# Decay attention and two MoE layers on one core: other homes and order for the first block's loads, and the second block's first steps placed behind the first products

## The chip, the cores and the metric

The kernel runs on 1 core of one Trainium2 chip (trn2). The metric is the device time of one execution in microseconds, the median of 3 runs. The inputs lie in the chip's memory, the weights as float64 numbers whose bytes the kernel converts itself.

## What is computed

```python
# q, k, v: (4 batches, 8 heads, 576, 64); f: (4, 8, 576)
scores = 1.0 / np.sqrt(64) * np.matmul(q, k.transpose(0, 1, 3, 2))
cum = np.cumsum(np.log(np.clip(f, 0.0001, 1.0)), axis=-1)
scores = np.where(causal, -1e9, scores + cum[:, :, :, None] - cum[:, :, None, :])
attn = exp(scores - max) / (sum + 1e-09)
x = np.matmul(attn, v) -> (2304 tokens, 512)
h = x @ w_in                      # 512 x 2048
x = np.maximum(0.01 * h, h) @ w_out   # 2048 x 512
out = ((x @ w_a) * (x @ w_b)) @ w_out2   # 512 x 1536, 1536 x 512
```

## The kernel before

**The work.** Products of the MoE layers run on TensorE in fp32r. Each operand is split into a high and a low part (xh and xl, w[:, 0] and w[:, 1]), and a product is three matmuls: high by high, low by high, high by low. The first MoE works on chunks of 256 tokens. For one chunk and one pair of weight groups (there are 16 groups, 8 pairs), l1 makes h_0, h_1, ... (L857, 24 matmuls of 128x256), ScalarE makes gh (L868) and hs (L869), VectorE gl (L871), and l2 adds to y (L886, 24 matmuls). Weights arrive in raw_a (L156), and ScalarE and VectorE turn them from bytes to fp32 and split them (c_a, w_a: L120, L125 on ScalarE, L121, L130, L167, L168 on VectorE).

**The attention.** It goes block by block; a block is a batch and a part of its tokens. The first block is tokens 0 to 255 of batch 0, the second the rest of batch 0. Heads come in pairs (0 to 3): both heads of a pair lie side by side in the 128 partitions. For a pair the steps are: load q, k (xq, xk), v (vn) and the scan of the logarithms (cumb); transpose q and k on TensorE (tq, tk) and copy them (qn, kn); scores on TensorE (s); the decay and the causal mask on GpSimd (p); scores and decay added with a row minimum on VectorE (L374); exp on ScalarE (L345); normalisation; transpose of the probabilities (pp) and a copy (ph); product with v (av); and the result split into xh (ScalarE) and xl (VectorE). The first chunk of the MoE is the first block's result, so h_0 needs xh and xl of all four pairs; the innermost loop of l1 begins with pair 3.

**What sets the order.** The first block's order is a list of words, FIRST (from L613): `lq0` loads q of pair 0, `lk`, `lv`, `lc` load k, v and the scan, `g1` a group of weights, `qT`, `kT` are the transposes, `Sa`, `Sb` scores, `D` the decay, `m` the mask, `M` the sum and minimum, `E` exp, `N` the normalisation, `T`, `h` the probabilities' transpose and copy, `V` the product with v, `xh`, `xl` the split, `ca` to `cf` the conversion of a group. InOrder (L593) chains each engine's instructions in this order, in_line (L145) the loads on SyncE's queue (L642 is `load`). In the text below V3 is the word V of pair 3, four matmuls in the order (eight records in the trace). The listed loads have high priority; other instructions are placed by a scheduler, by priority. Behind (L80) is a wrapper of an engine: each instruction given through it stands behind one instruction (`first`) in that engine's order. In the second block, heads 2 to 7 go through pe_held (behind the last matmul of h_0) and dve_held (behind xl of pair 3); heads 0 and 1 go free.

**Homes.** A tile's tag names its place in memory. Before, q of pairs 0 and 2 share the tag xq, pairs 1 and 3 xq2; the same holds for k (xk, xk2) and v (vs, vhl). So a load for pair 2 waits until pair 0's reader has finished, and the second block's tiles follow in the same tags.

Of the kernel before, what the change touches and what calls it, by code (L numbers as in the profile page):

```python
# [26 lines left out]
def kernel(  # L27
# [570 lines left out]
    class InOrder:  # L598
# [19 lines left out]
        cc0 kn0 Sa0 qn1 cd0 kT1 lq3 lk3 g3 lc3 D011 D001 Sb0 m011 m010 kn1 m001 ce0 M010 M000 M011 ca1 M001
        cf0 Sa1 D100 E011 Sb1 m100 D110 E010 M100 cb1 E000 D101 E001 D111 rec01 cc1 rec00 m101 qT2 N01 m110
        m111 kT2 N00 qn2 T01 M111 ca2 g4 kn2 T00 M110 D200 M101 E110 cb2 D211 Sa2 E111 m211 cd1 E101 Sb2  # L620
        D201 E100 m201 h01 qT3 D210 rec11 h00 m200 kT3 N10 m210 cc2 N11 V0 lv2 M200 M201 E200 M211 E201 M210
        ce1 T11 E211 D310 D300 qn3 kn3 T10 D301 E210 cf1 xh0 Sa3 m310 h11 m301 m300 Sb3 h10 xl0 D311 ca3 g5
        rec21 m311 M300 V1 lv3 N21 M310 E300 M311 E310 M301 E311 N20 T21 xh1 rec31 E301 T20 N31 h21 xl1 T31
        cd2 h20 V2 rec30 ce2 N30 cb3 T30 xh2 h31 xl2 h30 cc3 V3 cd3 xh3 xl3 cf2 ce3 cf3
# [221 lines left out]
    def l1(i, pr):  # L846
# [5 lines left out]
        for u in range(2):  # L852
            wih, wil = wa[2 * pr + u][0], wa[2 * pr + u][1]
            n = 0
            for c in reversed(range(ND)):
# [303 lines left out]
```

## Time and profile before

| | |
|---|---|
| median of 3 runs | 1079.65 us (1077.82 to 1080.82) |
| the profiled execution | 1078.16 us |
| its span in the profile | 1076.3 us |
| busy: PE, DVE, ACT, POOL | 1049.8, 553.8, 544.1, 205.3 us |
| mean granted clock of TensorE | 0.992 of full speed |

The span is counted from the first to the last instruction of the profiled execution; 1.86 us of its time lie outside. PE is TensorE (PEld its weight loads), DVE VectorE, ACT ScalarE, POOL GpSimd, SP SyncE, which only issues transfers here. A wait in brackets stands at the instruction that follows it and names what ended it. DMA rows of the chain of waits run from issue to landing.

### The profile page before, as it was taken

How to read it: one execution, taken by the hardware profiler on the slowest of the kernel's cores; microseconds unless marked ns; L12 is line 12 of the kernel's file. 1: busy time of each engine (PE TensorE's matmuls, PEld its weight loads, DVE VectorE, ACT ScalarE, POOL GpSimd, SP SyncE). 2: the span in 40 equal slices, each digit the busy share in tenths (PEclk: the TensorE clock that was granted, in tenths of full speed). 3: DMA queues.
4: the chain of work that ended last, by engine and by line, in shares of the span. 5: the costliest groups of instructions: out<-in, count | busy, mean ns of one | idle time of the engine just before them, and what ended most of it. 6: DMA issues, size and time to landing. Idle time of an engine off the chain costs nothing.

```text
span 1076.3 us, 19114 instructions
## 1 busy us (share of the span) xinstructions
PE 1049.8 (98%) x6945; PEld 944.0 (88%) x6945; DVE 553.8 (51%) x1290; ACT 544.1 (51%) x1212; POOL 205.3 (19%) x430
## 2 busy tenths in 40 slices
PE   5799999999999999999999999999999999999998
PEld 3577789999999999999999988888888888888897
DVE  5599767877788777767428684112112111211121
ACT  7588777967887868877435562112112111211121
POOL 4435323343343324233000001010002000100000
PEclk9799999999999999999999999999999999999999
DMA  8788245233553244321236662002001000100010
GB/s 239 198 259 239 44 93 113 48 92 67 103 105 66 64 87 105 77 51 34 79 98 206 224 196 59 1 5 75 1 1 50 20 1 1 50 0 1 1 40 20
DMA packets 185438, 86.40 MB, mean 80 GB/s; under 512 B 143808, under 2 KB 173248, under 8 KB 185344
## 3 DMA queue, kind: packets, MB, share of 16 engines
q1 hardware_dynamic: 179728, 79.34, 28.4%
q10 hardware_dynamic: 5616, 5.84, 1.6%
q8 instruction: 55, 0.90, 0.4%
q14 instruction: 39, 0.32, 0.1%
HBM read 75.63 MB, written 9.51 MB: 79 GB/s over the span
## 4 chain that ended last, share of the span: by engine, by line
PE 92%; DMA 3%; DVE 2%; issue 1%; POOL 0%; ACT 0%; SPq 0%; ACTq 0%; DVEq 0%; POOLq 0%
PE ab L955 27%; PE h L857 18%; PE y L886 18%; PE o L978 14%; PE s L76 5%; PE av L76 5%; PE pp L76 3%; DMA raw_a<-in_moe_w_out_dram 1%; DMA xq_f<-in_q_dram 1%; DVE c_a L130 0%; DMA vn_f<-in_v_dram 0%; DMA cumb_f<-cum_dram 0%; POOL p L390 0%; DVE p L90 0%; PE av_f L608 0%
## 5 line engine op out<-in xcount | busy, mean ns | idle before, releaser
L955 PE MATMUL ab<-yh,w_ab 128*128 128x512 f32 (+1 forms) x960 | 279.5, 367 | 0.0
L857 PE MATMUL h<-xh,w_a 128*128 128x256 f32 x1152 | 228.6, 284 | 1.2 <-ACT hs L869 1.2
L886 PE MATMUL y<-gh,w_a 128*128 128x256 f32 x1152 | 223.3, 282 | 1.6 <-ACT gh L868 1.6
L955 PEld LDWEIGHTS ab<-yh,w_ab 128*128 128x128 f32 x960 | 174.2, 188 | 30.4
L857 PEld LDWEIGHTS h<-xh,w_a 128*128 128x128 f32 x1152 | 185.3, 190 | 6.1 <-ACT hs L869 2.0
L961 DVE TENSOR_TENSOR p<-ab,p 128x512 f32<-128x512 f32 (+1 forms) x60 | 38.3, 638 | 291.0 <-PE ab L955 291.0
L886 PEld LDWEIGHTS y<-gh,w_a 128*128 128x128 f32 x1152 | 182.3, 188 | 5.4 <-ACT gh L868 2.2
L955 PE MATMUL ab<-yl,w_ab 128*128 128x512 f32 (+1 forms) x480 | 176.2, 367 | 0.0
L857 PE MATMUL h<-xl,w_a 128*128 128x256 f32 x576 | 163.1, 283 | 0.1
L886 PE MATMUL y<-gl,w_a 128*128 128x256 f32 x576 | 160.9, 281 | 0.1
L978 PE MATMUL o<-w_c,pph 128*128 128x512 f32 x432 | 142.7, 389 | 0.0
L960 ACT COPY p<-ab 128x512 f32<-128x512 f32 (+1 forms) x60 | 32.6, 544 | 179.9 <-PE ab L955 179.3
L857 PEld LDWEIGHTS h<-xl,w_a 128*128 128x128 f32 x576 | 109.3, 190 | 0.7 <-DVE xl L429 0.3
L886 PEld LDWEIGHTS y<-gl,w_a 128*128 128x128 f32 x576 | 108.3, 188 | 1.2 <-DVE c_a L121 0.5
L955 PEld LDWEIGHTS ab<-yl,w_ab 128*128 128x128 f32 x480 | 90.2, 188 | 15.3
L362 POOL TENSOR_SCALAR p<-cumb,ncum_t 128x384 f32<-128x384 f32 (+1 forms) x112 | 77.0, 695 | 138.1 <-PE pp L76 39.1
L111 ACT CAST pph<-p 128x512 fp32r<-128x512 f32 (+1 forms) x60 | 34.6, 577 | 127.7 <-DVE p L961 127.7
L978 PEld LDWEIGHTS o<-w_c,pph 128*128 128x128 f32 x432 | 81.1, 188 | 16.6
L345 ACT ACTIVATE p<-p,stat 128x384 f32<-128x384 f32 (+4 forms) x128 | 77.0, 603 | 33.8 <-DVE stat L374 25.0
L112 POOL TENSOR_TENSOR yl<-sy,yh 128x512 fp32r<-128x512 f32 (+1 forms) x16 | 19.2, 1210 | 390.0 <-ACT yh L111 252.9
L978 PE MATMUL o<-w_c,ppl 128*128 128x512 f32 x216 | 84.2, 390 | 0.0
L871 DVE TENSOR_TENSOR gl<-hs,gh 128x512 fp32r<-128x512 f32 x72 | 51.0, 708 | 41.6 <-ACT hs L869 41.1
(155 smaller groups left out, 1655.8 us busy)
## 6 DMA issues: line engine op xcount, KB each, us to landing
cumb<-cum_dram SPq DMA_DIRECT2D x32, 288.0 KB, 3.8
raw_a<-in_moe_w_out_dram SPq DMA_DIRECT2D x15, 511.6 KB, 5.9
raw_a<-in_moe_w_in_dram SPq DMA_DIRECT2D x15, 510.5 KB, 4.7
raw_c<-in_moe_w_out_dram SPq DMA_DIRECT2D x12, 511.6 KB, 5.3
raw_ab<-in_moe_w_a_dram SPq DMA_DIRECT2D x12, 510.5 KB, 5.7
raw_ab<-in_moe_w_b_dram SPq DMA_DIRECT2D x12, 510.5 KB, 6.6
xq<-in_q_dram SPq DMA_DIRECT2D x144, 32.0 KB, 2.1
y_dram<-yo ACTq DMA_DIRECT2D x18, 256.0 KB, 2.9
```

The costliest lines, as they stand in the source:

```text
L76: return method(*args, **kw)
L111: nc.scalar.copy(hi, src)
L112: (lo_engine or nc.gpsimd).tensor_tensor(out=lo, in0=src, in1=f32(hi), op=ALU.subtract)
L345: act_att.activation(pt, pt, AF.Exp, bias=stat[:, 0, s : s + 1], scale=-1.0, accum_out=stat[:, 1, s : s + 1])
L362: made = pool_att.tensor_scalar(pt, cumb[:, :n], 1.0, ncum_t[:, t, bh : bh + 1], op0=ALU.mult, op1=ALU.add)
L857: made = nc.tensor.matmul(hps[:, u, :], w[:, c * P : c * P + P], x[:, c, :], start=(n == 0), stop=(n == 3 * ND - 1))
L871: nc.vector.tensor_tensor(out=gl, in0=hs, in1=f32(gh), op=ALU.subtract)
L886: nc.tensor.matmul(o, w[:, d * P : d * P + P], g[:, u, :], start=(fi == 0 and n == 0 and d % 2 == 0), stop=(fi == NF1 - 1 and n == 2 and d ...
L955: nc.tensor.matmul(o[:, :tn], w[:, c * P : c * P + P], y[:, c, :tn], start=(m == 0), stop=(m == 3 * ND - 1))
L960: nc.scalar.copy(p[:, :tn], ab[0][:, :tn])
L961: nc.vector.tensor_tensor(out=p[:, :tn], in0=ab[1][:, :tn], in1=p[:, :tn], op=ALU.mult)
L978: nc.tensor.matmul(o, g[:, t * P : t * P + P], w, start=(fi == 0 and m == 0), stop=(fi == NF2 - 1 and m == 2))
```

## The change

There are three parts.

**Homes.** A new function `pairs` gives one tile to two pairs each of k (ks_f0, ks_f1) and v (vs_f0, vs_f1), in the tags that held one pair; q of pairs 2 and 3 gets a tile in the tag `tk` (qs_f1), in which the scan's ones lay. No load of the first block shares a place with another pair's tile any more.

**The loads' order.** All loads stand at the list's head, ahead of the first computing word; the computing words keep their order.

**The second block's heads 0 and 1.** Three new wrappers: pe_next and act_next (behind the last matmul of V3, and behind xh of pair 3) take the transposes of q and of the first half of k and their copies; pe_mid (behind the last matmul of h_0's first half) takes the transposes of k's second half and the scores.

```diff
-    pe_held, dve_held = Behind(pe_free), Behind(dve_free)
+    pe_held, dve_held, pe_next, act_next, pe_mid = (
+        Behind(e) for e in (pe_free, dve_free, pe_free, act_att, pe_free)
+    )
     def engines_of(b, r, h):
-        return (pe_held, dve_held) if (b, r) == (0, 1) and h >= 2 else (pe_free, dve_free)
+        if (b, r) != (0, 1):
+            return pe_free, dve_free, act_att
+        return (pe_held, dve_held, act_att) if h >= 2 else (pe_next, dve_free, act_next)
...
-        pe_att, dve_att = engines_of(b, r, h)
+        pe_att, dve_att, act_att = engines_of(b, r, h)
+        pe_late = pe_mid if pe_att is pe_next else pe_att
...
-                        pe_att.transpose(tk[:, ...
+                        (pe_late if c0 else pe_att).transpose(tk[:, ...
...
-                    pe_att.matmul(o[:n, u, : cols_.stop - cols_.start], ...
+                    pe_late.matmul(o[:n, u, : cols_.stop - cols_.start], ...
...
     FIRST = """
-        lq0 lk0 lq1 lk1 g1 cumT ncum lc1 lv0 g2 ca0 rep qT0 cb0 D000 D010 kT0 lq2 lk2 lc2 lv1 m000 qn0 qT1
+        lq0 lk0 lq1 lk1 g1 cumT ncum lv0 lk2 lq2 lc1 g2 lc2 lv1 lq3 lk3 lc3 g3 lv2 lv3 ca0 rep qT0 cb0 D000
...
+        def pairs(p, key, tags):
+            both = tile_of((key, p // 2), lambda: ap_.tile([P, 2, 2, 2, 64], F32, tag=tags[p // 2], name=f"{key}_f{p // 2}"))
+            return both[:, p % 2]
         def lq(p):
-            x = got["xq", p] = ap_.tile([P, 2, 2, 64], F32, tag=("xq", "xq2")[p % 2], name=f"xq_f{p}")
+            if p < 2:
+                x = ap_.tile([P, 2, 2, 64], F32, tag=("xq", "xq2")[p], name=f"xq_f{p}")
+            else:
+                x = pairs(p, "qs", (None, "tk"))
+            got["xq", p] = x
         def lk(p):
-            x = got["xk", p] = ap_.tile([P, 5, 2, 64], F32, tag=("xk", "xk2")[p % 2], name=f"xk_f{p}")
+            x = got["xk", p] = pairs(p, "ks", ("xk", "xk2"))
         def lv(p):
-            x = got["v", p] = ap_.tile([P, 5, 2, 64], F32, tag=("vs", "vhl")[p % 2], name=f"vn_f{p}")
+            x = got["v", p] = pairs(p, "vs", ("vs", "vhl"))
...
+            got["av", "end"] = made
...
             dve_held.first = made
+            pe_next.first, act_next.first = got["av", "end"], got["xh", p]
...
-                    if pe_held.first is None and u == 1 and n == 3 * ND - 1:
-                        pe_held.first = made
+                    for late_, half in ((pe_mid, 0), (pe_held, 1)):
+                        if late_.first is None and u == half and n == 3 * ND - 1:
+                            late_.first = made
```

On SyncE's queue, behind the loads of pairs 0 and 1's q and k and the first weights, there stood before (a digit behind `_f` is the pair, raw_a_2 and raw_a_3 are weight groups; v of pairs 2 and 3 followed some 20 rows on):

```order
L642 DMA cumb_f1_127<-cum_dram_58 128x256 x2
L642 DMA vn_f0_130<-in_v_dram 128x2x64 x2
L156 DMA raw_a_2_133<-in_moe_w_in_dram 128x4x1021
L156 DMA raw_a_2_133<-in_moe_w_out_dram 128x4093
L642 DMA xq_f2_153<-in_q_dram 128x2x64 x2
L642 DMA xk_f2_156<-in_k_dram 128x2x64 x2
L642 DMA cumb_f2_159<-cum_dram_58 128x256 x2
L642 DMA vn_f1_162<-in_v_dram 128x2x64 x2
L642 DMA xq_f3_184<-in_q_dram 128x2x64 x2
L642 DMA xk_f3_187<-in_k_dram 128x2x64 x2
L156 DMA raw_a_3_190<-in_moe_w_in_dram 128x4x1021
L156 DMA raw_a_3_190<-in_moe_w_out_dram 128x4093
```

Now there stands (vs_f0 and ks_f1 are the tiles of two pairs, 0 and 1 or 2 and 3):

```order
L647 DMA vs_f0_126<-in_v_dram 128x2x64 x2
L647 DMA ks_f1_129<-in_k_dram 128x2x64 x2
L647 DMA qs_f1_132<-in_q_dram 128x2x64 x2
L647 DMA cumb_f1_135<-cum_dram_58 128x256 x2
L160 DMA raw_a_2_138<-in_moe_w_in_dram 128x4x1021
L160 DMA raw_a_2_138<-in_moe_w_out_dram 128x4093
L647 DMA cumb_f2_141<-cum_dram_58 128x256 x2
L647 DMA vs_f0_126<-in_v_dram 128x2x64 x2
L647 DMA qs_f1_132<-in_q_dram 128x2x64 x2
L647 DMA ks_f1_129<-in_k_dram 128x2x64 x2
L647 DMA cumb_f3_150<-cum_dram_58 128x256 x2
L160 DMA raw_a_3_153<-in_moe_w_in_dram 128x4x1021
L160 DMA raw_a_3_153<-in_moe_w_out_dram 128x4093
L647 DMA vs_f1_156<-in_v_dram 128x2x64 x4
```

The q and k of pair 2 have moved ahead of the scan rows of pair 1 (cumb_f1) and of the weights raw_a_2, the scan rows of pair 3 ahead of raw_a_3, and all v have come up to the other loads.

On PE, around V3 (av_f3) and the first product (h_0_0; names with `0_1_0` are the second block's heads 0 and 1), there stood before:

```order
L608 MATMUL pp_f3_0_462<-ident_65,p_f3_0_357 128x128 x3
L76 MATMUL tq_0_1_0_586<-ident_65,xq_0_1_0_576 128x128 x2
L76 MATMUL tq_0_1_0_586<-ident_65,xk_0_1_0_577 128x64
L76 MATMUL tk_0_1_0_0_591<-ident_65,xk_0_1_0_577 128x128 x2
L608 MATMUL av_f3_473<-ph_f3_0_470,vn_f3_411 64x256
L76 MATMUL tk_0_1_0_2_595<-ident_65,xk_0_1_0_577 128x128 x2
L76 MATMUL tk_0_1_0_2_595<-ident_65,xk_0_1_0_577 128x64
L608 MATMUL av_f3_473<-ph_f3_1_467,vn_f3_411 64x256
L608 MATMUL av_f3_473<-ph_f3_0_470,vn_f3_411 64x128
L608 MATMUL av_f3_473<-ph_f3_1_467,vn_f3_411 64x128
L76 MATMUL s_0_1_0_2_609<-kn_0_1_0_575,qn_0_1_0_574 128x384 x2
L857 MATMUL h_0_0_485<-xh_0_370,w_a_0_211 128x256
```

Now there stands:

```order
L613 MATMUL pp_f3_0_457<-ident_65,p_f3_0_355 128x128 x3
L613 MATMUL av_f3_468<-ph_f3_0_465,vs_f1_156 64x256
L613 MATMUL av_f3_468<-ph_f3_1_462,vs_f1_156 64x256
L613 MATMUL av_f3_468<-ph_f3_0_465,vs_f1_156 64x128
L613 MATMUL av_f3_468<-ph_f3_1_462,vs_f1_156 64x128
L76 MATMUL tq_0_1_0_581<-ident_65,xq_0_1_0_571 128x128 x2
L76 MATMUL tq_0_1_0_581<-ident_65,xk_0_1_0_572 128x64
L76 MATMUL tk_0_1_0_0_586<-ident_65,xk_0_1_0_572 128x128 x2
L873 MATMUL h_0_0_480<-xh_0_368,w_a_0_212 128x256
```

V3 is no longer divided, and of the second block only the transposes tq and the first tk stand ahead of the first product.

Right behind the 24 matmuls of h_0 there now stands on PE:

```order
L76 MATMUL tk_0_1_0_2_590<-ident_65,xk_0_1_0_572 128x128 x2
L76 MATMUL tk_0_1_0_2_590<-ident_65,xk_0_1_0_572 128x64
L76 MATMUL tq_0_1_2_629<-ident_65,xq_0_1_2_619 128x128 x2
L76 MATMUL tq_0_1_2_629<-ident_65,xk_0_1_2_620 128x64
L76 MATMUL tk_0_1_2_0_634<-ident_65,xk_0_1_2_620 128x128 x2
L903 MATMUL y_0_0_542<-gh_0_0_506,w_a_0_212 128x256
L903 MATMUL y_0_1_543<-gh_0_0_506,w_a_0_212 128x256
L873 MATMUL h_0_1_511<-xh_0_368,w_a_2_452 128x256
```

The second tk has moved here. The first head's matmul of s_0_1_0_2 follows behind the last matmul of h_1 (h_0_1), and the second head's behind 22 matmuls of y more; both stood ahead of h_0 before.

## Rows read from the trace of the kernel before

**Rows 1.** The page's busy times; share of the span, number of instructions.
```profile
PE 1049.8 (98%) x6945; PEld 944.0 (88%) x6945; DVE 553.8 (51%) x1290; ACT 544.1 (51%) x1212; POOL 205.3 (19%) x430
```

**Rows 2.** By stretch: us, busy (instructions) by engine, granted clock, DMA share, GB/s.
```profile
10.00:20.00 10.00, 5.03 (x23) 2.58 (x21) 7.38 (x25) 7.16 (x16) 5.45 (x12) 1.00 1.00 290
...
40.00:45.00 5.00, 3.61 (x13) 1.72 (x15) 0.88 (x1) 0.73 (x3) 0.08 (x1) 0.50 0.95 265
...
60.00:120.00 60.00, 57.28 (x396) 44.02 (x394) 56.87 (x117) 51.71 (x100) 29.94 (x36) 1.00 0.73 205
120.00:142.00 22.00, 22.00 (x155) 17.45 (x155) 13.10 (x39) 13.46 (x35) 5.75 (x15) 0.93 0.18 39
150.00:250.00 100.00, 100.00 (x837) 99.26 (x836) 76.31 (x216) 79.26 (x202) 36.07 (x90) 1.00 0.41 87
```

**Rows 3.** Chain of waits, first 60 us: start us, us, what.
```profile
8.33 4.73 DMA raw_a<-in_moe_w_out_dram
...
13.08 6.32 DMA xq_f<-in_q_dram
...
22.89 4.70 DMA cumb_f<-cum_dram
...
36.41 4.85 DMA vn_f<-in_v_dram
...
42.48 0.92 PE tk L76 x3
...
44.86 1.58 PE s L76 x4
```

**Rows 4.** PE timeline: start us, us, instructions, [idle before and releaser].
```profile
19.54 0.66 PE L608 MATMUL tqk_f<-ident,xq_f 128*128 128x128 f32 x2 [3.05 <-DMA xq_f<-in_q_dram]
...
35.30 1.96 PE L608 MATMUL av_f<-ph_f,vn_f 128*64 128x256 f32 x8 [0.79 <-DVE c_a L608]
...
41.39 1.08 PE L608 MATMUL av_f<-ph_f,vn_f 128*64 128x256 f32 x2 [1.96 <-DMA vn_f<-in_v_dram]
...
46.38 0.58 PE L857 MATMUL h<-xh,w_a 128*128 128x256 f32 x1
46.76 0.41 PE L857 MATMUL h<-xl,w_a 128*128 128x256 f32 x1
...
48.03 0.32 PE L857 MATMUL h<-xl,w_a 128*128 128x256 f32 x1
...
49.95 0.28 PE L857 MATMUL h<-xh,w_a 128*128 128x256 f32 x1
```

**Rows 5.** POOL timeline, same columns.
```profile
22.24 1.87 POOL L608 TENSOR_SCALAR p_f<-cumb_f,ncum_t 128x128 f32<-128x128 f32 x1
...
27.78 2.23 POOL L608 TENSOR_SCALAR p_f<-cumb_f,ncum_t 128x128 f32<-128x128 f32 x3 [3.18 <-DMA cumb_f<-cum_dram]
```

**Rows 6.** DVE timeline, same columns.
```profile
22.73 1.22 DVE L608 SCALAR_TENSOR_TENSOR c_a<-raw_a,c_a 128x1024 int32<-128x1024 int32 x1
...
30.78 0.29 DVE L608 CUSTOM_DVE_ANT_0 p_f<-s_f,p_f 128x128 f32<-128x128 f32 x1 [1.00 <-POOL p_f L608]
...
45.30 0.43 DVE L608 TENSOR_TENSOR xl<-av_f,xh 128x256 fp32r<-128x256 f32 x1 [4.43 <-ACT xh L608]
...
49.93 0.56 DVE L374 CUSTOM_DVE_ANT_0 p<-s,p 128x384 f32<-128x384 f32 x1 [0.90 <-POOL p L365]
```

**Rows 7.** ACT timeline, same columns.
```profile
37.56 1.10 ACT L608 COPY ph_f<-pp_f 128x384 f32<-128x384 f32 x2
...
44.90 0.37 ACT L608 CAST xh<-av_f 128x256 fp32r<-128x256 f32 x1 [1.04 <-PE av_f L608]
```

**Rows 8.** PE timeline around 92 us, upper clock level.
```profile
91.95 0.92 PE L76 MATMUL s<-kn,qn 64*128 64x384 f32 x4
92.79 0.64 PE L76 MATMUL tk<-ident,xk 128*128 128x128 f32 x3
```

**Rows 9.** PE timeline, the longest wait between 60 and 142 us.
```profile
119.18 0.50 PE L886 MATMUL y<-gh,w_a 128*128 128x256 f32 x2 [1.62 <-ACT gh L868]
```

More of the change, by code (lines that the diff above doesn't have):

```diff
@@ L273, in att_scores @@
                         w = min(P, nk - c * P)
-                        pe_att.transpose(tk[:, (c - c0) * P : (c - c0) * P + w], xk[:w, c, :, :].rearrange("p u d -> p (u d)"), ident[:w, :w])
+                        (pe_late if c0 else pe_att).transpose(tk[:, (c - c0) * P : (c - c0) * P + w], xk[:w, c, :, :].rearrange("p u d -> p (u d)"), ident[:w, :w])
                     k1 = min(c1 * P, nk)
@@ L282, in scores_of_both @@
                     n, at = min(P, nq - z), slice(u * 64, u * 64 + 64)
-                    pe_att.matmul(o[:n, u, : cols_.stop - cols_.start], qn[at, z : z + n], kn[at, cols_], start=True, stop=True)
+                    pe_late.matmul(o[:n, u, : cols_.stop - cols_.start], qn[at, z : z + n], kn[at, cols_], start=True, stop=True)
             q_at = 0
@@ L616 @@
     FIRST = """
-        lq0 lk0 lq1 lk1 g1 cumT ncum lc1 lv0 g2 ca0 rep qT0 cb0 D000 D010 kT0 lq2 lk2 lc2 lv1 m000 qn0 qT1
[L618 to L624, printed above, removed]
+        lq0 lk0 lq1 lk1 g1 cumT ncum lv0 lk2 lq2 lc1 g2 lc2 lv1 lq3 lk3 lc3 g3 lv2 lv3 ca0 rep qT0 cb0 D000
+        D010 kT0 m000 qn0 qT1 cc0 kn0 Sa0 qn1 cd0 kT1 D011 D001 Sb0 m011 m010 kn1 m001 ce0 M010 M000 M011
+        ca1 M001 cf0 Sa1 D100 E011 Sb1 m100 D110 E010 M100 cb1 E000 D101 E001 D111 rec01 cc1 rec00 m101 qT2
+        N01 m110 m111 kT2 N00 qn2 T01 M111 ca2 g4 kn2 T00 M110 D200 M101 E110 cb2 D211 Sa2 E111 m211 cd1
+        E101 Sb2 D201 E100 m201 h01 qT3 D210 rec11 h00 m200 kT3 N10 m210 cc2 N11 V0 M200 M201 E200 M211 E201
+        M210 ce1 T11 E211 D310 D300 qn3 kn3 T10 D301 E210 cf1 xh0 Sa3 m310 h11 m301 m300 Sb3 h10 xl0 D311
+        ca3 g5 rec21 m311 M300 V1 N21 M310 E300 M311 E310 M301 E311 N20 T21 xh1 rec31 E301 T20 N31 h21 xl1
+        T31 cd2 h20 V2 rec30 ce2 N30 cb3 T30 xh2 h31 xl2 h30 cc3 V3 cd3 xh3 xl3 cf2 ce3 cf3
     """
@@ L649, in lk @@
         def lk(p):
-            x = got["xk", p] = ap_.tile([P, 5, 2, 64], F32, tag=("xk", "xk2")[p % 2], name=f"xk_f{p}")
+            x = got["xk", p] = pairs(p, "ks", ("xk", "xk2"))
             for u in range(2):
-                load(x[:, :2, u, :], k[0, 2 * p + u, : 2 * P, :].rearrange("(c p) d -> p c d", p=P))
+                load(x[:, :, u, :], k[0, 2 * p + u, : 2 * P, :].rearrange("(c p) d -> p c d", p=P))
         def lv(p):
-            x = got["v", p] = ap_.tile([P, 5, 2, 64], F32, tag=("vs", "vhl")[p % 2], name=f"vn_f{p}")
+            x = got["v", p] = pairs(p, "vs", ("vs", "vhl"))
             for u in range(2):
-                load(x[:, :2, u, :], v[0, 2 * p + u, : 2 * P, :].rearrange("(c p) d -> p c d", p=P))
+                load(x[:, :, u, :], v[0, 2 * p + u, : 2 * P, :].rearrange("(c p) d -> p c d", p=P))
         def lc(p):
```

## The prediction

> **What bounds the kernel now.** The first view is the page's line of busy times: PE works 98% of a span of 1076.3 us [rows 1]. From 150 us on it is busy in each of 100 us of 100 [rows 2], at the granted clock 1.00, the upper of the two levels (2.4 GHz). The change touches nothing behind that point but the clock time at which PE reaches it. The question is therefore one of the first 150 us: how much earlier does PE come to its unbroken run of products?
>
> The second view, busy time by stretches, shows three stages there. Until about 46 us the first block is computed, and PE is not full: 3.61 us of 5 between 40 and 45 us, at a clock of 0.50, the lower level (1.2 GHz) [rows 2]. From 60 to 120 us PE (57.28 of 60) and DVE (56.87) are both nearly full, since the weights are converted there beside the second block's attention. From 120 to 142 us PE is full and DVE is not (13.10 of 22).
>
> The third view, the chain of waits, says what the first stage waited for: a load of weights until 13.06, then xq_f (pair 2's q, landed at 19.40), cumb_f (pair 3's scan rows, 27.59) and vn_f (pair 3's v, 41.26) [rows 3]. The timelines tell who stood idle: PE 3.05 us for xq_f [rows 4], POOL 3.18 us for cumb_f [rows 5] and DVE 1.00 us behind POOL [rows 6], PE 1.96 us for vn_f [rows 4]. The first product of pair 0 stands at 46.38 [rows 4].
>
> **The loads.** The change orders the queue anew and gives each pair a home. Rates first: in 10 to 20 us the DMA engines moved 290 GB/s at a share of 1.00 [rows 2]. After 13.06 us the queue now holds 0.39 MB up to pair 2's q (six loads of 64 KB), so an estimate from that rate is 14.4 us instead of 19.40. Up to pair 3's scan rows it holds 2.62 MB (9.0 us): 22.1 instead of 27.59. Up to the last v it holds 3.93 MB (13.6 us): 26.6 instead of 41.26. The weights that land at 13.06 stand in front in both orders, so nothing here can come before them. The second block's first q and k fall behind the next weights (1.05 MB more, about 30.3) and are used behind V3 only, so that costs nothing; qs of pairs 2 and 3 waits for a tile that DVE's scan leaves before 7 us, ahead of their place in the queue. The price: pair 1's scan rows now stand behind v of pair 0 (which followed them), and q and k of pair 2, 0.39 MB or 1.4 us later, and POOL waits for them.
>
> **The first product.** V3 (the values of pair 3) waits for three things: its v, its ph copies and PE. The copies end at 37.56 + 1.10 = 38.66 [rows 7]. With v long there and nothing between, V3 takes what V2 took for the same work, 1.96 us [rows 4], so it ends at 40.7 (0.1 for the hand-over); xh follows with 0.37 [rows 7], and the first product, which needs xh alone, stands at 41.2. That is 5.2 us earlier than 46.38; xl's 0.43 [rows 6], which the second product needs, costs some 0.2 that the rounding holds. What of the earlier waits goes comes on top. DVE's 1.00 goes whole, since the scan rows are 5 us earlier. Of PE's 3.05 I take 1.0: pair 1's scan rows are 1.4 us late, and the streams of ACT and DVE that follow are not empty. The bounds are 0 and 4.05; 2.0 is nearest to what DVE, the busiest engine there, loses by itself. So the first product stands at 39.2: **-7.2 us** (bounds -5.2 and -9.3).
>
> POOL's decay of pair 3 moves from 27.78 into about 23 us. There one such piece took 1.87 us [rows 5], while DVE ran a 1.22 us operation on two inputs [rows 6]; at 27.78 three took 2.23, or 0.74 each. The Trainium skill ("SBUF — State Buffer", Who interferes with whom) says that VectorE with two SBUF inputs and a GpSimd instruction that reads SBUF exclude each other on a shared port, the later one being blocked whole. The 1.87 agrees with it; by that rule one meeting more costs about 1.1 us (1.87 less 0.74), and the sum would be 1.1 us less of a gain. The bounds above hold that without it.
>
> **What was moved behind.** The second tk (0.92) and the scores of heads 0 and 1 (1.58) [rows 3] no longer stand ahead of the first product; that is in the 5.2. They come back at the upper clock at 0.64 and 0.92 [rows 8]: **+1.6 us**.
>
> **The clock.** The first 24 products ran from 46.38 to 50.23 (49.95 + 0.28), 3.85 us: from the second to the eighth (46.76 to 48.03) 0.212 us apart, then 0.12 apart (48.03 to 49.95, sixteen steps) [rows 4]. PE had worked without a break from 41.39 when the step changed. With the products 7 us earlier and a thinner stretch ahead of them, I take the lower level for all 24: 24 x 0.212 = 5.1, **+1.2 us**. Bounds: -1.0 if the clock is up from the start (24 x 0.12 = 2.9), +2.4 if it stays down for twelve products more.
>
> So PE leads by 7.2 - 1.6 - 1.2 = **4.4 us** behind the first 24 products.
>
> **What the next stage leaves of it.** Two things have to keep the lead. The products follow the weights' conversions, which also start earlier, since DVE and ACT stood idle around 40 to 45 us (DVE 0.88 busy of 5) [rows 2]; for them the lead is 4.4. The second block's own steps follow its scores, and these now stand behind pair 1's products: 39.2 + 5.1 + 1.7 for eight transposes (0.64 for three [rows 8]) + 3.1 for 26 products at 0.12 = 49.1, and the first head's score ends at 49.6 (half of 0.92). DVE took that score at 49.93 before, having waited 0.90 for POOL [rows 6]. So the second block's lead is only 0.3 us. DVE does both in turn, with 3.1 us free in 60. ACT's qn and kn of heads 0 and 1 move behind xh3 too; those scores are all that waits for them. The end of the stage therefore lies between -4.4 and 0; PE must have the last pair of the second block before its next 256 tokens' products can start. I take the middle: 2.4 of the 4.4 given back.
>
> **Sum:** -7.2 + 1.6 + 1.2 + 2.4 = **-2.0 us**. The profiled execution took 1078.16 us and the sum makes it 1076.2; it lay 1.49 below the median of the runs shown (1079.65), so the median is forecast at **1077.65 us**.
>
> **Rivals.**
> *The lead is kept.* Conversions pace the stage alone, and the second block's later scores fit between them. For it: PE stood idle for only 2.7 us of 60 to 120 and DVE is only 60% busy from 120 to 142 [rows 2], room to catch up. Against it: DVE's 95%. It gives -4.4: 1075.3; with the clock up early -6.6: 1073.1.
>
> *The lead is all lost.* DVE's 56.87 of 60 us is the pace, and what PE gains it waits for later. For it: DVE's work in the stage is the same, and it can't subtract gl of pair 0 before that pair's h is there. Against it: DVE's idle of 4.1 us in 40 to 45, which goes. It gives 0: 1079.65. That the reordered loads only exchange one wait for another (scan rows of pair 1 for q of pair 2) would end here too, but V3's wait would still go.
>
> *Slower: the second block's chain is late and PE stops for it.* Its place is 100 to 142 us: later scores of heads 0 and 1 push exp, normalisation and values of all four pairs, and PE, which leads by its products, runs out of them. Before, such a stop at 119.18 cost 1.62 us of waiting [rows 9], and the granted clock of 120 to 142 was 0.93 [rows 2], 7% of 22 or 1.5 us: 3.1 together. Two stops more than before cost 6.3, and 2.0 of lead remains: +4.3, 1083.9. It decides from the point where new waits of PE exceed 2.0 + 3.2 = 5.2 us. Against it: a PE that leads also has y products to fill in.
>
> **How the numbers follow.** A difference under 0.3%, 3.24 us, can hardly be told from no change here; the bounds are 1076.4 and 1082.9. Forecast (lead partly kept, -0.5 to -3.2): 0.43. Lead kept: 0.31. All lost: 0.13. Slower: 0.13. Faster takes the lead kept and a small part of the forecast's own spread, 0.33; slower 0.13; the rest, 0.54, is no change. The range reaches from -7.2 (the first product's whole gain, all kept) to +3.4, into the slower rival: 1072.5 to 1083.0.
>
> **What would show it.** In the profile after: xq_f's successor (qs_f) lands near 14.4 us and PE's 3.05 wait is gone or under 1.5; POOL's wait for pair 3's scan rows is gone; V3 is undivided and starts near 36.8; the first product stands at 38.5 to 40; its 24 take 4 to 5.2 us; PE's idle from 60 to 142 us grows from 2.7 to about 5. A first product later than 41.2 would say that the loads' step failed; a granted clock of 1.00 ahead of the first product, that the clock's did; PE idle of 8 us and more between 60 and 142, that the second block's chain decides. An end below 1075 would say that the give-back was wrong.

## The result and the profile after

| | before | after |
|---|---|---|
| median of 5 runs each | 1078.70 us (1076.47 to 1080.82) | 1086.47 us (1083.92 to 1087.67) |
| the profiled execution | 1078.16 us | 1085.94 us |
| its span | 1076.3 us | 1084.2 us |

The ratio is 1.0064, with an interval of 1.0047 to 1.0080: **slower by 0.6%**, some 7 us, where 2 us less were forecast. It lies outside the range.

The page's busy times of after; [rows 1] answers to them:

```profile
PE 1054.6 (97%) x6945; PEld 946.5 (87%) x6945; DVE 551.6 (51%) x1290; ACT 545.6 (50%) x1212; POOL 199.9 (18%) x430
```

The same instructions, but PE is 4.8 us longer busy, and the stretches below show where the lower clock made them longer.

By stretch (columns as in [rows 2], POOL's busy time fifth, then the granted clock):

```profile
50.00:60.00 10.00, 10.00 (x69) 8.02 (x69) 6.04 (x10) 4.17 (x9) 0.00 (x0) 1.00 0.93 278
60.00:120.00 60.00, 53.91 (x345) 40.64 (x345) 53.33 (x105) 48.21 (x88) 21.14 (x28) 0.91 0.64 188
120.00:142.00 22.00, 22.00 (x154) 16.58 (x152) 8.92 (x31) 14.23 (x35) 8.04 (x19) 1.00 0.21 46
```

From 60 to 120 us PE is busy for 53.91 us, where it was 57.28, and the granted clock is 0.91 where it was 1.00 [rows 2]. DVE, which was to be the pace, is busy less than before, 53.33 where it was 56.87. So nobody is full: the engines wait for each other. And just ahead, from 50 to 60 us, where PE still works through its lead, DVE is busy for 6.04 of 10 and ACT for 4.17.

PE's timeline of after (start, time, instructions, in brackets the idle time before and its releaser):

```profile
16.02 0.69 PE L613 MATMUL tqk_f<-ident,qs_f 128*128 128x128 f32 x2
...
36.98 0.87 PE L613 MATMUL av_f<-ph_f,vs_f 128*64 128x256 f32 x8 [0.62 <-ACT ph_f L613]
...
39.52 0.39 PE L873 MATMUL h<-xh,w_a 128*128 128x256 f32 x1 [0.74 <-DVE xl L613]
...
43.87 0.28 PE L873 MATMUL h<-xh,w_a 128*128 128x256 f32 x1
43.99 0.58 PE L76 MATMUL tk<-ident,xk 128*128 128x128 f32 x3
...
49.01 0.91 PE L76 MATMUL s<-kn,qn 64*128 64x384 f32 x2
...
52.63 0.91 PE L76 MATMUL s<-kn,qn 64*128 64x384 f32 x2
...
61.61 0.27 PE L873 MATMUL h<-xh,w_a 128*128 128x256 f32 x1
63.95 2.47 PE L76 MATMUL s<-kn,qn 64*64 64x288 f32 x4 [2.06 <-DVE stat L379]
...
106.36 0.50 PE L903 MATMUL y<-gh,w_a 128*128 128x256 f32 x2 [1.94 <-ACT gh L885]
...
146.17 0.28 PE L873 MATMUL h<-xh,w_a 128*128 128x256 f32 x1
```

V3 is whole and starts at 36.98, and the first product stands at 39.52, 6.86 us earlier than at 46.38 [rows 4]. The last row is the first product of the next 256 tokens, chunk 1 (the 385th product recorded). Before, it stood here:

```profile
142.21 0.28 PE L857 MATMUL h<-xh,w_a 128*128 128x256 f32 x1
```

The lead at the same count of products is therefore 6.9 us at the first, 5.6 at the 49th (48.68 against 54.28), **-4.0 at chunk 1's first**, and -7.8 at the last product of the first MoE (642.68 against 634.88). The rest of the kernel keeps that.

From the first product to chunk 1's first PE needed 106.65 us, before 95.83. The 10.8 us between them are worked out from the whole timelines: PE's gaps sum to 7.35 us, before 2.72 (4.6 more); the granted clock is 0.50 for 13.65 us, before for 5.14, and 8.5 us more at half speed cost 4.3; and the second tk and the scores of heads 0 and 1, now behind the first product, take 0.58 and, head by head, twice 0.84 (49.01 to 49.84, 52.63 to 53.47), or 2.3. Together that is 11.2, some 0.4 more than the 10.8 to be explained: the clock's term is an estimate, and 0.2 us of idle time at the lower clock stand in it twice.

Two stops carry most of it, 63.95 with 2.06 us and 106.36 with 1.94. The clock falls at both, as the windows of after show (the first row is the stretch of the first products):

```profile
39.86:43.25 3.39, 3.39 (x18) 3.39 (x17) 3.35 (x4) 1.18 (x1) 3.39 (x2) 0.50 0.84 267
...
57.00:63.70 6.70, 4.46 (x30) 3.17 (x28) 4.78 (x7) 4.39 (x8) 0.00 (x0) 1.00 0.94 277
63.75:70.55 6.80, 6.61 (x20) 4.13 (x20) 5.60 (x15) 5.58 (x11) 0.00 (x0) 0.50 0.79 261
...
108.13:111.50 3.37, 3.37 (x12) 1.42 (x12) 3.37 (x6) 2.64 (x5) 0.00 (x0) 0.50 0.00 0
```

Behind the first the lower level (1.2 GHz) lasts 6.8 us, behind the second 3.4. If all of that is put down to the stops, they cost 2.06 + 3.4 = 5.5 and 1.94 + 1.7 = 3.6 us, against 1.62 + 1.7 = 3.3 for the one long stop of before [rows 9] (its clock was at 0.50 from 119.8 to 123.2). That the stops pulled the clock down is read from their nearness alone; E7 and E9 below have a stop without a fall, and a fall without such a stop.

**The first stop, step by step.** PE's score at 63.95 waits for DVE's L379, the sum and minimum of the scores before it (x4, the 512-wide third part of heads 0 and 1, made at 57.77); the score's home in PSUM is free only then. DVE's timeline of after says why it came so late:

```profile
53.69 0.56 DVE L379 CUSTOM_DVE_ANT_0 p<-s,p 128x384 f32<-128x384 f32 x1 [0.49 <-PE s L76]
...
54.65 0.08 DVE L379 DVE_READ_ACCUMULATOR2_ANT stat<- 128x1 f32 x1
54.65 0.69 DVE L171 CAST w_a<-c_a 128x1024 fp32r<-128x1024 f32 x1
58.57 0.69 DVE L125 TENSOR_SCALAR c_a<-c_a 128x1024 f32<-128x1024 f32 x1 [3.23 <-ACT c_a L124]
59.18 1.22 DVE L172 TENSOR_TENSOR w_a<-c_a,w_a 128x1024 fp32r<-128x1024 f32 x1
60.72 1.23 DVE L134 SCALAR_TENSOR_TENSOR c_a<-raw_a,c_a 128x1024 int32<-128x1024 int32 x1 [0.32 <-ACT c_a L129]
61.98 0.69 DVE L171 CAST w_a<-c_a 128x1024 fp32r<-128x1024 f32 x1
62.59 0.68 DVE L379 CUSTOM_DVE_ANT_0 p<-s,p 128x512 f32<-128x512 f32 x1
```

DVE stood idle for 3.23 us before the clamp of weight group 6 (L125), and the sums stand behind that clamp and two more steps of the same group (L134, L171). In the order of before they stand ahead of all three, as DVE's timeline of before shows (the second sum follows at 60.09):

```profile
59.48 0.68 DVE L374 CUSTOM_DVE_ANT_0 p<-s,p 128x512 f32<-128x512 f32 x1
...
60.70 0.69 DVE L121 TENSOR_SCALAR c_a<-c_a 128x1024 f32<-128x1024 f32 x1
```

The rows of DVE's queue, before (c_a_6 and w_a_6 are group 6, p_0_1_0_3 and p_0_1_1_3 heads 0 and 1's third part):

```
98 L374 ISA p_0_1_0_3_652,stat_0_1_0_573<-s_0_1_0_3_657,p_0_1_0_3_652 128x512
100 L374 ISA p_0_1_1_3_661,stat_0_1_0_573<-s_0_1_0_3_657,p_0_1_1_3_661 128x512
102 L121 TENSOR_SCALAR c_a_6_856<-c_a_6_856 128x1024
109 L130 SCALAR_TENSOR_TENSOR c_a_6_856<-raw_a_6_677,c_a_6_856 128x1024
114 L167 CAST w_a_6_861<-c_a_6_856 128x1024
```

and after:

```
99 L125 TENSOR_SCALAR c_a_6_851<-c_a_6_851 128x1024
101 L134 SCALAR_TENSOR_TENSOR c_a_6_851<-raw_a_6_672,c_a_6_851 128x1024
102 L171 CAST w_a_6_856<-c_a_6_851 128x1024
103 L379 ISA p_0_1_0_3_647,stat_0_1_0_568<-s_0_1_0_3_652,p_0_1_0_3_647 128x512
105 L379 ISA p_0_1_1_3_656,stat_0_1_0_568<-s_0_1_0_3_652,p_0_1_1_3_656 128x512
```

ACT's timeline of after shows the same one engine further up, with group 6's first step (L124) ahead of the exps of heads 0 and 1:

```profile
54.15 0.43 ACT L281 COPY kn<-tk 128x320 f32<-128x320 f32 x1 [3.00 <-PE tk L76]
57.41 1.13 ACT L124 ACTIVATE c_a<-raw_a 128x1024 f32<-128x1024 int8 x1 [2.83 <-DMA raw_a<-in_moe_w_out_dram]
58.44 0.60 ACT L90 ACTIVATE p<-p,stat 128x384 f32<-128x384 f32 x1
```

The minimum that the exp needs was read at 54.65, the exp ran at 58.44. Its engine was idle, but stood before an instruction that waited for weights. These are group 6's weights. They were issued at 51.56 and landed at 57.30; in the trace of before the same transfer was issued at 51.04 and landed at 57.85. So PE led by 5.6 us, but the weights by 0.55 only. In the kernel their fetch stands behind group 4's first step on ACT (L124), and that ended at 42.09. What stood ahead of it then was SyncE's own queue: from 47.21 on it issued loads of the second block one after the other, each in about 0.5 us. SP's timeline of after:

```profile
49.74 0.58 SPq L452 DMA_DIRECT2D vn<-in_v_dram  x1
50.37 0.51 SPq L454 DMA_DIRECT2D vn<-in_v_dram  x1
50.98 0.53 SPq L160 DMA_DIRECT2D raw_a<-in_moe_w_in_dram  x1
51.56 0.50 SPq L160 DMA_DIRECT2D raw_a<-in_moe_w_out_dram  x1
```

Before it was the same: group 4's first step had ended at 48.18, and the queue issued without a break from 45.41 until group 6's turn came at 50.61. (The chain of waits names ACT's L129 as what released the issue; that step ended at 51.15, after the first of the two issues had begun.)

**The second stop** has the same form on ACT: gh, which PE waits for at 106.36, ran at 105.69 behind two conversion steps that filled the 2 us ahead of it.

```profile
103.71 1.06 ACT L129 ACTIVATE c_a<-c_a 128x1024 int32<-128x1024 f32 x1
104.67 1.16 ACT L124 ACTIVATE c_a<-raw_a 128x1024 f32<-128x1024 int8 x1
105.69 0.62 ACT L885 ACTIVATE gh<-h 128x512 fp32r<-128x512 f32 x1
```

### The profile page after: what moved, and what is told of

Read it like the earlier page. It is cut to its first block, busy times and chain, and to the rows that moved or that the text cites. A ratio compares the mean times of both kernels' runs of the same rounds, so it can differ in the third digit from the quotient of the medians.

```text
span 1084.2 us, 19093 instructions
## 1 busy us (share of the span) xinstructions
PE 1054.6 (97%) x6945; PEld 946.5 (87%) x6945; DVE 551.6 (51%) x1290; ACT 545.6 (50%) x1212; POOL 199.9 (18%) x430
## 4 chain that ended last, share of the span: by engine, by line
PE 89%; DVE 4%; DMA 3%; ACT 3%; issue 1%; SPq 0%; ACTq 0%; DVEq 0%
PE ab L972 27%; PE h L873 18%; PE y L903 17%; PE o L995 14%; PE s L76 5%; PE av L76 5%; PE pp L76 3%; DMA raw_a<-in_moe_w_out_dram 3%; DVE c_a L134 0%; DMA xk<-in_k_dram 0%; ACT p L388 0%; DVE p L90 0%; ACT gh L885 0%; DVE w_a L172 0%; ACT p L350 0%
## 5 line engine op out<-in xcount | busy, mean ns | idle before, releaser
L903 PE MATMUL y<-gh,w_a 128*128 128x256 f32 x1152 | 225.7, 283 | 1.9 <-ACT gh L885 1.9
L367 POOL TENSOR_SCALAR p<-cumb,ncum_t 128x384 f32<-128x384 f32 (+2 forms) x112 | 76.3, 690 | 148.0 <-PE pp L76 51.8
L350 ACT ACTIVATE p<-p,stat 128x256 f32<-128x256 f32 (+3 forms) x123 | 73.4, 598 | 34.8 <-DVE stat L379 22.9
```

What stands on the lines that cost most here:

```text
L350: act_att.activation(pt, pt, AF.Exp, bias=stat[:, 0, s : s + 1], scale=-1.0, accum_out=stat[:, 1, s : s + 1])
L367: made = pool_att.tensor_scalar(pt, cumb[:, :n], 1.0, ncum_t[:, t, bh : bh + 1], op0=ALU.mult, op1=ALU.add)
L903: nc.tensor.matmul(o, w[:, d * P : d * P + P], g[:, u, :], start=(fi == 0 and n == 0 and d % 2 == 0), stop=(fi == NF1 - 1 and n == 2 and d ...
```

## The experiments

Four theories. **A**: the loss comes from the moved scores. The scheduler places other work where they no longer stand, so that group 6's conversion comes ahead of the second block's sums and exps (narrow: that place in the queues does it; wide: the scores' distance itself). **B**: the loads do it. **C**: the late part of the loss, the 3.8 us behind chunk 1's start, comes from the other order that the scheduler chose there. **D**: it isn't order at all. Each run below was timed in five rounds; "lead" is against the trace of before at the same count of products, and a negative lead is lateness.

**E1: the loads and homes alone**, the second block free as before.

```diff
-        if (b, r) != (0, 1):
-            return pe_free, dve_free, act_att
-        return (pe_held, dve_held, act_att) if h >= 2 else (pe_next, dve_free, act_next)
+        return (pe_held, dve_held, act_att) if (b, r) == (0, 1) and h >= 2 else (pe_free, dve_free, act_att)
```

> The loads' homes and order alone; heads 0 and 1 of the second block go free as before. Theory A (the moved scores are the loss: on DVE the conversion of weight group 6 comes to stand ahead of the second block's sums and minima, and waits for weights there): faster than before by 2 to 6 us, 1073 to 1077; first product near 42 us, PE idle from 60 to 142 us under 3 us. Theory B (the loads are the loss: the new order or the earlier conversions run into weights that land no earlier): slower than before by 3 to 8 us, like the changed kernel.

Measured 1077.95 us, ratio 0.9990 (0.9977 to 1.0004). The first product stands at 42.73, and chunk 1 starts at 136.08, 6.1 us early. From 60 to 120 us the profile of E1 reads:

```profile
60.00:120.00 60.00, 59.26 (x412) 46.24 (x411) 56.21 (x108) 48.76 (x92) 30.05 (x36) 1.00 0.73 204
```

PE is fuller than before. B falls. But of the 6.1 us only 1.9 are left at the last product of the first MoE, and the median can't be told from no change, where A had named 2 to 6 us of gain. A part of that goes at 143.3 us, where PE stops for 1.50 us and the clock is at 0.50 for the next 3.4.

**E2: the scores' places alone**, with the loads and homes of before (the first block's list is the old one, the wrappers are the new ones).

> The second block's heads 0 and 1 behind the products alone; loads, homes and their order as before. Theory A: slower than before by 3 to 9 us, 1082 to 1088, with DVE waiting ahead of the second block's 128x512 sums for a conversion of group 6 and PE stopping behind it. Theory B: within 2 us of before.

Measured 1083.83 us, ratio 1.0043 (1.0029 to 1.0058). DVE's queue around group 6 has the order of after, the clamp ahead of the sums, yet the first stop is not there; DVE's timeline of E2:

```profile
59.19 0.68 DVE L125 TENSOR_SCALAR c_a<-c_a 128x1024 f32<-128x1024 f32 x1
...
62.88 0.68 DVE L379 CUSTOM_DVE_ANT_0 p<-s,p 128x512 f32<-128x512 f32 x1
```

The clamp waits for nothing. Without the lead DVE comes to it when its weights are there. The second stop is there:

```profile
104.44 0.50 PE L895 MATMUL y<-gh,w_a 128*128 128x256 f32 x2 [1.93 <-ACT gh L877]
```

So the new places, with the order that follows from them, cost 0.4% by themselves. The sums come at 62.88 in E2 and at 62.59 in the changed kernel: what the loads add as a lead seems to go into the first stop, which is argued from the two traces and not shown by a run.

**E3: the second tk and the scores ahead of the first product again**, all else changed.

```diff
-        pe_late = pe_mid if pe_att is pe_next else pe_att
+        pe_late = pe_att
```

> The changed kernel, but the second tk and the scores of heads 0 and 1 stand right behind V3 and the first tk, ahead of the first product, instead of behind the first half of h_0. Theory A: as the loads alone, faster than before by 2 to 6 us; the first product about 42 us, 2.5 later than in the changed kernel, and PE idle from 60 to 142 us under 3. Theory B: slower than before by 3 to 8 us like the changed kernel.

Measured 1078.39 us, ratio 0.9988 (0.9974 to 1.0001); chunk 1 starts at 137.76. The loss is gone with the distance.

**E4: group 6's load issued right behind group 5's.**

```diff
-        ca3 g5 rec21 m311 M300 ...
+        ca3 g5 g6 rec21 m311 M300 ...
...
-                fetch_a(behind=got["ca", n - 2])
+                fetch_a(behind=got["ca", min(n - 2, 3)])
```

> The changed kernel, but the load of weight group 6 is issued right behind that of group 5, some 10 us earlier; all else in the kernel's text is the same. Theory A in its narrow form (the conversion of group 6 that stands ahead of the sums costs because its weights land at 57.3): ACT's wait of 2.83 us and DVE's of 3.23 us around 57 us go, PE's stop of 2.06 us at 63.95 shrinks by 1 us or more, and the time falls by 2 to 5 us, to 1081.5 to 1084.5. Theory A in its wide form (any product ahead of the scores costs): within 1.5 us of the changed kernel. Theory B: falls by 4 us and more.

Measured 1085.28 us, ratio 1.0055 (1.0037 to 1.0073): a miss of the narrow form's range. The time is within 1.5 us of the changed kernel, as the wide form had it, but the trace does not decide: group 6's weights landed by 46.87, and the first stop is gone, yet two others stand there, of 2.67 us at 47.47 and of 3.26 us at 81.74. PE's timeline of E4:

```profile
47.47 0.66 PE L76 MATMUL tq<-ident,xq 128*128 128x128 f32 x2 [2.67 <-DMA xq<-in_q_dram]
```

For the first of them the weights had taken the place of the second block's q.

**E5 and E6: the order of before, held from chunk 1's first product to chunk 3's** on every engine and on SP, on top of E1 (E5) and of the changed kernel (E6). PINNED lists the numbers of the instructions in before's order.

```diff
+    for queue in PINNED.split(";"):
...
+        for a, b in zip(names, names[1:]):
+            tc.add_manual_dep(by_name[b], a, ORDER, reason="as in the kernel before")
```

> The loads' homes and order alone (the second block's heads free), and from the first product of chunk 1 to that of chunk 3 every engine's instructions and SyncE's transfers in the order that the kernel before has there, written out as dependencies. Loads alone led by 6.1 us at chunk 1's first product and by 1.9 at the end of the first MoE. Theory C (the late loss of some 4 us is the scheduler's other order behind chunk 1's start): the loss goes to under 1.5 us, and the time falls to 1073 to 1075.5, 0.3 to 0.5% under before. Theory D (the late loss is what an earlier arrival costs, whatever the order: weights, transfers or the clock): within 1.5 us of the loads alone.

> The changed kernel with the same order written out from chunk 1's first product to chunk 3's. It lost 4.0 us at chunk 1's first product against before and 7.8 by the end. Theory C: 1081 to 1084, some 3 to 4 us less than the changed kernel; the lead lost until chunk 1, 4 us, stays. Theory D: within 1.5 us of the changed kernel.

E5 measured 1077.17 us, ratio 0.9981 (0.9969 to 0.9994), E6 1086.93 us, 1.0066 (1.0051 to 1.0081). E5 is within 1.5 us of E1 and E6 of the changed kernel, as D had it; C is not confirmed.

**E7: the second tk ahead of the first product, the scores where the change has them.** They then need nothing that comes later and follow h_0's 24 products at once, at 42.12 instead of 49.01 and 52.63.

```diff
-                        (pe_late if c0 else pe_att).transpose(tk[:, ...
+                        pe_att.transpose(tk[:, ...
```

> The changed kernel, but the second tk of heads 0 and 1 stands ahead of the first product, so that both scores come right behind h_0 instead of behind h_1 and 22 products of y. If the distance of the scores from the first product is what costs (theory A, wide): most of the loss until chunk 1 goes, chunk 1's first product at 136 to 141 us instead of 146, and the time falls by 5 to 8 us to 1078 to 1081. If any step behind a product costs as much: within 2 us of the changed kernel.

Measured **1076.94 us, ratio 0.9977 (0.9964 to 0.9991)**: faster than before. The first product stands at 39.12, chunk 1 starts at 136.85, 5.4 us early, and at the end of the first MoE 2.9 are left. Both heads' scores run side by side again, in 0.92 us, where the changed kernel spent that on each of them. DVE still waits for group 6's clamp, but only this one step of the group stands ahead of the sums, which run 3.0 us earlier than at 62.59. DVE's timeline of E7:

```profile
57.84 0.69 DVE L125 TENSOR_SCALAR c_a<-c_a 128x1024 f32<-128x1024 f32 x1 [2.74 <-ACT c_a L124]
...
59.58 0.68 DVE L379 CUSTOM_DVE_ANT_0 p<-s,p 128x512 f32<-128x512 f32 x1
```

Of the stop at 64 us 0.59 are left, and the one at 106 is gone. E7 isn't free of stops, though; PE's timeline of E7 has two others:

```profile
42.12 0.92 PE L76 MATMUL s<-kn,qn 64*128 64x384 f32 x4
45.04 0.66 PE L76 MATMUL tq<-ident,xq 128*128 128x128 f32 x2 [2.00 <-issue]
...
76.99 1.73 PE L76 MATMUL av<-ph,vn 128*64 128x256 f32 x16 [1.71 <-ACT ph L487]
```

At the first the clock fell to 0.50 for 6.8 us, as at the first stop of the changed kernel; at the second it stayed at 1.00.

**E8: the changed kernel with the sums and exps ahead of group 6**: ACT's first step of the group ordered behind the last exp of heads 0 and 1, DVE's clamp behind their last sum.

```diff
...
+    first, clamp = kept["group", 6]
+    tc.add_manual_dep(first.ins, kept["exp", 0, 1, 1, 1].ins.name, ORDER, reason="group 6 behind heads 0 and 1")
+    tc.add_manual_dep(clamp.ins, kept["sum", 0, 1, 1, 1].ins.name, ORDER, reason="group 6 behind heads 0 and 1")
```

> The changed kernel, scores and loads as there, but on ScalarE the first step of weight group 6 stands behind the second block's exps of heads 0 and 1, and on VectorE behind their sums and minima. Theory A, narrow (both engines stand idle some 3 us around 57 us behind a conversion whose weights land at 57.3, while ready steps of heads 0 and 1 queue behind it): PE's stop of 2.06 us at 63.95 shrinks to under 0.7, the half-clock stretch of 63.7 to 70.6 goes, and the time falls by 3 to 6 us. Theory A, wide (the scores themselves are late): within 2 us of the changed kernel, with the stop at another place.

Measured 1080.63 us, ratio 1.0008 (0.9997 to 1.0019). PE's score that had waited 2.06 us, in the timeline of E8:

```profile
61.56 1.37 PE L76 MATMUL s<-kn,qn 64*64 64x288 f32 x4
```

It comes at 61.56 without a wait. Two ordered pairs bring back about 6 of the 7 us, by the ratios (1.0064 less 1.0008). The scheduler's later order changed with them: the second stop is gone, and two smaller ones (1.31 us at 76.36, 1.67 at 97.35) have come; the clock is still at 0.50 from 65.5 to 68.9, for 3.4 us instead of 6.8. So what E8 shows is the place of group 6 together with what the scheduler makes of it.

**E9: DVE's half of E8 alone**, ACT's first step left free.

```diff
...
+    first, clamp = kept["group", 6]
+    tc.add_manual_dep(clamp.ins, kept["sum", 0, 1, 1, 1].ins.name, ORDER, reason="group 6 behind heads 0 and 1")
```

> As the experiment in which group 6's conversion stands behind the sums and exps of heads 0 and 1 (1080.6 us), but on VectorE alone: ScalarE keeps the first step of group 6 ahead of the exps, as in the changed kernel. If VectorE's queue is what held the second block up (its sums free the scores' bank, for which PE stopped at 63.95): 1079.5 to 1082. If ScalarE's queue is (the exps behind a conversion that waits for its weights): within 2 us of the changed kernel, 1084.5 and more.

Measured 1080.92 us, ratio 1.0017 (1.0008 to 1.0026). About 5 us come back, so DVE's order, with what the scheduler makes of it, carries most. Both stops of the changed kernel are gone, but not the lower clock: it is at 0.50 for 6.8 us from 65.42, behind waits of 0.33 and 0.38 us only. So the 5 us can't be put down to the first stop and its clock. ACT's half alone was not tried.

**E11: E7's places with the loads and homes of before.**

> The second tk ahead of the first product and the scores right behind h_0 (1076.9 us with the new loads), but with the loads, their homes and order of the kernel before. If the new loads carry the gain of that version: 1078.5 to 1081, no gain over before. If the place of the scores carries it and the loads add nothing: within 1 us of 1076.9.

Measured **1075.73 us, ratio 0.9975 (0.9964 to 0.9985)**, the fastest median. Its first product stands only at 44.44, yet chunk 1 starts at 136.97, as in E7:

```profile
60.00:120.00 60.00, 59.56 (x427) 47.29 (x425) 57.05 (x116) 50.99 (x97) 25.94 (x34) 1.00 0.69 196
```

PE's 57.28 of 60 [rows 2] have become 59.56. From the first product to chunk 1 PE's gaps sum to 0.44 us, where E7 has 4.46 and the changed kernel 7.35. With the scores in this place the loads add nothing that these runs can tell: E7's interval is nearly the same.

**E12: E7 with before's later order**, held as in E5.

> The second tk ahead of the first product (1076.9 us), and from chunk 1's first product to chunk 3's the order of the kernel before, written out. Theory C in what is left of it (the other order behind chunk 1's start costs 1 to 2 us): 1074.5 to 1076.3. Theory D: within 1 us of 1076.9.

Measured 1084.85 us, ratio 1.0045 (1.0028 to 1.0061). The order of before doesn't fit a kernel that comes to it early. In PE's timeline of E12 a stop stands there that E7 has not (and another of 1.69 us at 147.42):

```profile
144.85 0.27 PE L76 MATMUL ppx<-ident,x 64*128 64x64 f32 x1 [1.91 <-ACT x L573]
```

C, as a loss that before's order would save, falls.

**What stays open.** Of the changed kernel's 7.8 us at the end of the first MoE, 4.0 are there when chunk 1 starts. The other 3.8 come later, and every variant, leading or late, loses between 2.3 and 4.3 us from its 481st product (about 160 us) to that end against the trace of before. A part could lie in the one trace compared with, which at 1078.16 us was a quicker execution than before's medians in these comparisons (1079.01 to 1079.61). Another part can be worked out from the timelines. From the 481st product to the end PE's gaps sum to 1.57 us in the changed kernel and to nothing before; the other 2.3 of its 3.9 us there are longer steps of the same matmuls at a clock of 1.00, and why they are longer no run shows. In E7 and E11 eleven records of the attention's matmuls more stand in this stretch, an estimated 1.3 us by their mean steps, so a part of their lead was work put off. Pinning the order (E5, E6, E12) didn't take the loss away.

## Why the prediction was wrong, point by point

**The loads: right in what they set free, the size in part by luck.** Pair 2's q no longer holds PE up: the transposes at 16.02 wait for nothing, where 3.05 us were waited [rows 4]. DVE's wait of 1.00 us for POOL is gone. V3 is undivided and starts at 36.98 (36.8 was named). The first product moved by -6.9 us (forecast -7.2, bounds -5.2 and -9.3). But two terms behind this were off, in opposite directions. V3 took 0.87 us at a clock of 1.00, where 1.96 was taken from a row at 0.50. And the first product didn't need xh alone: it waited for xl (the row at 39.52), which stood behind a conversion step of 1.22 us on DVE, so it came 1.7 us behind V3's end, where 0.5 was summed.

The landings were later than the 290 GB/s gave, but for pair 2's q at 14.82 us (14.4). Pair 3's scan rows landed at 26.40 (22.1), 1.2 us earlier than before and not 5, the last v at 30.46 (26.6), and pair 1's scan rows came 2.9 us later, not 1.4. What PE no longer waited at 16 us it waited behind it: pair 3's scores start at 27.76, only 0.2 us earlier than before (27.96), where 1.0 was taken for PE's wait.

The 1.1 us that the Trainium skill ("SBUF — State Buffer", Who interferes with whom) would have taken off for one meeting more is not seen: after as before there are two such meetings in this stretch, at other instructions. Before, a piece of 128x128 took 1.87 us [rows 5], and three at 27.78 took 2.23. After, a piece of 128x256 at 22.57 took 1.43, where another took 0.48 at 29.66, and three masks at 27.92 took 1.75, where three took 0.78 at 19.31. Beside them two-input steps of DVE took 1.31 (at 22.35) and 1.41 (at 27.62) instead of 1.22. This agrees with the rule in kind. The 1.87 us do so less than the prediction says: that piece had begun at 22.24, ahead of DVE's step at 22.73 [rows 6], and the rule blocks the later one. POOL's timeline of after:

```profile
22.57 1.43 POOL L613 TENSOR_SCALAR p_f<-cumb_f,ncum_t 128x256 f32<-128x256 f32 x1
...
27.92 1.75 POOL L613 TENSOR_SCALAR_AFFINE_SELECT p_f<-p_f 128x128 f32<-128x128 f32 x3
```

**The clock: the size right, the reason not.** The 24 products took from 39.52 to 44.15, 4.63 us (forecast 5.1, bounds 2.9 and up). I had taken the lower level as lasting from the thin stretch ahead; in fact the clock stood at 1.00 for the 3.4 us before 39.85, fell just as PE was full, and rose at 43.26.

**What was moved behind: the scores' price was too low.** The second tk took 0.58 us (forecast 0.64). The 0.92 of the scores was read from a row in which both heads run side by side [rows 8]. Here 22 products stand between the two heads, and each took that long by itself (the rows at 49.01 and 52.63), 1.7 us together. PE led by 5.6 us behind the first 24 products; less the scores, which it had still to pay, that is 3.9, where 4.4 were forecast.

**"What the next stage leaves of it": wrong, and this is the step that failed.** I took 2.4 us given back, bounded by "between -4.4 and 0", that is, by the lead itself. Counted from the 3.9, 7.9 us were given back by chunk 1's start, and 11.7 by the end of the first MoE. The bound rested on two leads, of the conversions and of the second block's scores. The second was wrong in itself: "the second block's lead is only 0.3 us" counted on the first head's score alone. That was there in time, at 49.84, but DVE's sum waited for the second head's score and ran at 53.69, where it ran at 49.93 before [rows 6]: 3.8 us late. (In E8 it is as late, at 54.12, and most of the loss is gone.) And the two leads were put together as if each kept its own: that DVE does both in turn was said, but not in which order. Both stand in one queue on DVE and in one on ACT, and each of these runs in its order. I asked when the scores would come and when the conversions could start; I didn't ask which would stand ahead of which, though the order of DVE shows group 6's three steps changing places with the sums. Nor did I ask whether the weights would lead as well. For the conversions "the lead is 4.4", I wrote; for group 6 it was 0.55. A late score then didn't cost its lateness but a stop of PE with a clock that stayed down for 6.8 us.

**The rivals.** "The second block's chain is late and PE stops for it" named the mechanism, with two stops of 1.62 + 1.5 and a chance of 0.13. Two stops stand there, at 5.5 and 3.6 us with the clock, against the one of before at 3.3; that is 5.8 more, where 6.3 were named for two more. The first is at 64 us, ahead of the stretch of 100 to 142 that it named. Its price of 1083.9 is 2.6 under the measured 1086.5. The argument against it, that a leading PE has y products to fill in, failed: from 50 to 60 us PE was full [the stretches above], and from 61.88 it stood idle. Of the signs, PE's idle time from 60 to 142 was named as 8 us and more for this case; it is 6.1 (53.91 of 60 and 22.00 of 22), and the lower clock did the rest.

**What the runs add.** E2 shows that the new places alone cost 0.4%, E1 that the loads alone are no loss, E8 and E9 that the order around group 6, with the scheduler's later order, takes most of the loss with it, E7 and E11 that the same scores 10 us nearer to the first product make it a gain. How much of the loss is the stop at 64 us itself stays open.

## What to carry to other kernels

A lead on one engine is worth only what the slowest landing leaves of it: for every instruction that now comes earlier, look whether what it waits for comes earlier too, and what stands behind it in its queue. Where a scheduler fills the gaps, moving one step far back changes the places of others; read the order of the busiest elementwise engine for conversions or loads' consumers that have passed ahead of what PE waits for. Here leaving one transpose ahead turned a ratio of 1.0043 (E2) into 0.9975 (E11), while loads that brought the first product 3.7 us earlier (E1) gave nothing that the runs can tell.

## What the runs showed of the hardware

- A short stop can be followed by more loss from the clock than it costs itself: 2.06 us of waiting at 63.95, with 6.8 us at 0.50, which is 3.4 us of work lost. After the stop of 1.94 us at 106.36 the lower level lasted 3.4 us. It is no rule: behind E7's stop of 1.71 us at 76.99 the clock stayed at 1.00, and in E9 it fell for 6.8 us behind waits of 0.33 and 0.38 us.
- Two score matmuls on different halves of the partitions ran in the time of one: 0.92 us for both heads together (E7, 42.12), 0.91 for each alone in the changed kernel (49.01, 52.63).
- The same 24 products took 4.63 us in the changed kernel and 3.07 in E7 (39.12 to 42.19, at 1.00), 0.4 us earlier and behind nearly the same instructions:

```profile
39.12:42.12 3.00, 3.00 (x24) 2.87 (x24) 2.97 (x3) 1.31 (x2) 2.90 (x3) 1.00 0.89 288
45.04:51.80 6.76, 6.76 (x29) 5.86 (x30) 4.08 (x8) 4.27 (x9) 2.90 (x9) 0.50 0.59 149
```

  In E7 the clock fell only at 45.01, after 2.0 us in which PE had stood still.
- POOL and DVE slowed each other at 39.85. Of the three decay pieces in the first row below (it prints the first one's shape for all) the first, 128x384, took 1.95 us, the second, 128x512, 2.17, both beside w_a steps of DVE, which took 1.43 and 1.41 instead of 1.22. The third, 128x512 too, took 0.69, nearly all of it with DVE idle, and at 97.03 one of 128x384 took 0.60. POOL's timeline of after:

```profile
39.85 4.78 POOL L367 TENSOR_SCALAR p<-cumb,ncum_t 128x384 f32<-128x384 f32 x3
...
97.03 0.60 POOL L367 TENSOR_SCALAR p<-cumb,ncum_t 128x384 f32<-128x384 f32 x1 [4.13 <-PE tq L76]
```

  The rule of the Trainium skill that the prediction cites ("SBUF — State Buffer", Who interferes with whom) has one block the other whole. POOL's pieces lost 1.35 and 1.48 us, about a whole step of DVE, which agrees; that DVE's steps grew as well, by 0.2 us each, the rule doesn't give. No run tried what it costs here.
